# Slices of 1024 for the experts' weights, squares on ScalarE and another order of products in the first FFN chunk

## The chip, the core and the metric

The kernel runs on one core of one Trainium2 chip. The metric is the device time of one execution in microseconds. The kernel before takes 599.48 us, the median of 3 runs (598.98 to 600.8).

## The reference

Three stages follow each other: attention with four sink keys and a window of 128, a mixture of eight experts with one expert for each token, and an FFN with squared relu. In numpy, cut to what matters here:

```python
x = attention(q, k, v, n_sink, window)                   # (1536, 512)
expert_idx = np.argmax(x @ w_gate, axis=1)               # each token goes to one expert
h = np.maximum(np.einsum('ecd,edf->ecf', disp, w1), 0.0) # disp: the tokens of expert e; w1 (8, 512, 1024)
y = np.einsum('ecf,efd->ecd', h, w2)                     # w2 (8, 1024, 512)
out[i] = gate_w[i] * y[expert_idx[i], pos[i]]
r = np.maximum(out @ w_in, 0.0)                          # w_in (512, 2048), float64 in memory
return ((r * r) @ w_out).astype(np.float32)              # w_out (2048, 512), float64 in memory
```

## The kernel before

All products are done in pieces of float32 precision: every operand is kept as a high part (a cast to fp32r, made on ScalarE) and a low part (what the cast left, subtracted on VectorE), and three products are summed: high x high, high x low, low x high. So all weights have to be split before they are used, beside the products that run.

**Experts.** `body(e, b)` computes 128 tokens of expert e: `g1` (12 products for each half of the 1024 hidden columns), `relu` (L927), `tr` (four transposes, then hTh cast on ScalarE, L938, and hTl subtracted on VectorE, L939), `g2` (24 products into y), then ys = y x gate on VectorE (L981) and an indirect DMA on the POOL queue that scatters ys into yd (L982). Block 0 of each expert is a full body; `more` adds block 1 and 2 under a branch if the expert has more than 128 or 256 tokens. In the full body of expert e the weights of expert e + 1 are split: eight slices of 128x1024 (four of w1, four of w2), in 16 halves of 512. `split` casts a half on ScalarE (L144, into xh or yh; experts of even number are x, of odd number y) and subtracts on VectorE (L145, into xl or yl). The table HEAVY says how many halves stand at each of six places in the body; what is left comes last. `pre` transposes the tokens of the next blocks and splits them (xT0, xT1; L707, L708).

**Buffers.** Raw weights lie in six slots of 128x1024 float32 (tiles raw). A slot is free when the subtraction that reads it is done, and the SP queue then issues the next load in a fixed order: weights of experts, then the pieces of w_in and w_out.

**FFN.** w_in and w_out come as float64 words. A piece (128 rows x 1024 values, two slots, 1 MB) is converted in four steps (`piece_stage`): 0, ScalarE scales the high words (L180) and VectorE shifts the low words (L181); 1, two bit operations on VectorE (L183, L184); 2, ScalarE casts the high part (L186: xh for w_in, yh for w_out); 3, VectorE subtracts the low part (L188: xl, yl). One `tick` does 2 and 3 of the older piece and 0 and 1 of the newer, in the order 2, 0, 3, 1. The first three ticks lie in the last expert, the others one in each step of the first chunk of the FFN. The pieces come in the order i0, i1, o0, i2, o1, i3, ... o6, o7 (i: w_in, o: w_out).

The FFN takes 512 tokens at a time (three chunks). A step is one block of 128 hidden units: `stage_a` (12 products into a), relu on ScalarE (L1139), the square on VectorE (L1140), then `stage_g`: gh (or xT0h) cast on ScalarE (L1155), gl (or xT0l) subtracted on VectorE (L1157); then a tick if pieces are left, in some steps a transposed block of the next chunk (L1040, L1045, L1046), and `stage_b` of the step before: for each of four token tiles the products gh x yh, gh x yl, gl x yh (L1196), each tile in a PSUM bank of its own. A step's stage_b needs the piece of w_out whose steps 2 and 3 were done one step earlier or before.

All queues work in the order in which the code issues. On SP stand, at the head of the FFN, 12 writes of zeros into the output (L1116), then three loads of yd (L1034), between the loads of pieces.

Of the kernel before, what the change touches and what calls it, by code (L numbers as in the profile page):

```python
# [8 lines left out]
F32 = mybir.dt.float32  # L9
# [3 lines left out]
AF = mybir.ActivationFunctionType  # L13
# [3 lines left out]
P = 128  # L17
# [1 line left out]
NOBODY = 8192  # L19
NWARM0 = 10  # L20

HEAVY = (3, 1, 2, 2, 0, 4)
LIGHT = (1, 1, 1, 1, 1, 1)
LAST = (0, 0, 1, 0, 1, 1)
NWARM = 2
PTACT = (0, 2)
SPOOL = ()
SDVE = ()
FILL = {0: 4, 1: 4, 2: 2, 3: 2}


# [1 line left out]
def kernel(  # L33
# [15 lines left out]
    nc = tc.nc  # L49
# [8 lines left out]
    NFF = FF // P  # L58
# [56 lines left out]
    def freed(n=1):  # L115
        nonlocal held
        held -= n
        if eager:
            pull(NRAW)

    class Weights:
# [19 lines left out]
        def split(self, n, eng=None, hi=None):  # L141
            i, sl = n // 2, slice(n % 2 * 512, n % 2 * 512 + 512)
            t = self.raw[i]
            (hi or nc.scalar.copy)(self.h[i][:, sl], t[:, sl])  # L144
            (eng or nc.vector).tensor_sub(self.l[i][:, sl], t[:, sl], self.h[i].bitcast(F32)[:, sl])  # L145
            if n % 2:
                freed()

# [754 lines left out]
    def body(e, b, splits, plan, also):  # L905
        xh, xl = xT[e, b]
        wts = W[e]
        splits = list(splits)

        def sp(n):  # L910
            for _ in range(n):
                if splits:
                    splits.pop(0)()

        hs = mp.tile([P, F], F32, tag="hs", name="hs", bufs=1)
        hp = [None, None]

        def g1(half, ks):
            if ks[0] == 0:
                hp[half] = ps("s" if half or b else "iv", "h")  # L920
            for kk in ks:
                r = slice(half * 512, half * 512 + 512)
                for m, (a, bb) in enumerate(((xh, wts.h), (xh, wts.l), (xl, wts.h))):
                    nc.tensor.matmul(hp[half], a[:, kk, :], bb[kk][:, r], start=(kk == 0 and m == 0), stop=(kk == KD - 1 and m == 2))

        def relu(half):
            nc.scalar.activation(hs[:, half * 512 : half * 512 + 512], hp[half], AF.Relu)  # L927

        hT = [None, None]

        def tr(half):
            p_ = ps("pt", "hT")
            for c in range(4):
                o0 = half * 512 + c * P
                nc.tensor.transpose(p_[:, c * P : (c + 1) * P], hs[:, o0 : o0 + P], ident)
            h_ = mp.tile([P, 512], F32R, tag="hTh", name="hTh", bufs=2)
            l_ = mp.tile([P, 512], F32R, tag="hTl", name="hTl", bufs=2)
            nc.scalar.copy(h_, p_)  # L938
            nc.vector.tensor_sub(l_, p_, h_.bitcast(F32))  # L939
            hT[half] = (h_, l_)  # L940

        y = ps("ot", "y")

        def g2(fs):
            for f in fs:
                h_, l_ = (x[:, (f % 4) * P : (f % 4 + 1) * P] for x in hT[f // 4])
                wh, wl = wts.h[KD + f // 2], wts.l[KD + f // 2]
                r = slice((f % 2) * 512, (f % 2) * 512 + 512)
                for m, (a, bb) in enumerate(((h_, wh), (h_, wl), (l_, wh))):
                    nc.tensor.matmul(y, a, bb[:, r], start=(f == 0 and m == 0), stop=(f == NF - 1 and m == 2))  # L950

        def point(i):
            for f in also.get(i, ()):
                f()

        plan = iter(plan)
        g1(0, [0, 1, 2, 3])
        sp(next(plan))
        relu(0)
        g1(1, [0, 1])  # L960
        sp(next(plan))
        tr(0)
        g1(1, [2, 3])
        sp(next(plan))
        relu(1)
        point(0)
        g2([0, 1])
        sp(next(plan))
        tr(1)
        point(1)  # L970
        g2([2, 3])
        point(2)
        sp(next(plan))
        g2([4, 5])
        point(3)
        g2([6, 7])
        point(4)
        sp(next(plan))
        y_ = mp.tile([P, DM + 1], F32, tag="ys", name="ys", bufs=2)
        nc.gpsimd.tensor_copy(y_.bitcast(I32)[:, DM:], src[:, b, e : e + 1])  # L980
        nc.vector.tensor_scalar(y_[:, :DM], y, gate_at(e, b), None, op0=ALU.mult)  # L981
        nc.gpsimd.indirect_dma_start(  # L982
            out=yd[:, :], out_offset=bass.IndirectOffsetOnAxis(ap=dst[:, b, e : e + 1], axis=0), in_=y_, in_offset=None,
            bounds_check=NTOK - 1, oob_is_err=False,
        )
        sp(len(splits))
# [25 lines left out]
    stream += [(2, lambda p_=p_: piece_load(p_)) for p_ in order]  # L1012
    eager = True
    pull(NRAW)

    def split_at(g, i):
        W[g].split(i, nc.gpsimd if i in SPOOL else None, nc.vector.tensor_copy if i in SDVE else None)


    CH = 512  # L1020
# [54 lines left out]
    for e in range(E):  # L1075
        g = e + 1
        if e > 0:
            W[g].alloc()
        for b in range(1, XB):
            load_x(e + 1, b)  # L1080
        if g < E:
            splits = [(lambda i=i, g=g: split_at(g, i)) for i in range(16)]
        else:
            splits = [ticks.tick] * (NPRE + 1)
            its = load_y(0, ("bg", "bg"))
        if nblk:
            also = {2: [lambda: pre(e, 1), lambda: pre(e + 1, 0), lambda: load_x(e + 2, 0)]}
            also[4] = its[:-1]
            body(e, 0, splits, HEAVY if g < E else LAST, also)
            if nblk > 1:  # L1090
                vals[e] = nc.values_load(cnt[0:1, e : e + 1], min_val=0, max_val=cap)
            more(e, 1, its[-1:])
        else:
            for f in splits + its:
                f()
# [25 lines left out]
    def stage_a(c, f):  # L1121
        nonlocal its
        if f == 0:
            its = load_y(c + 1, ("pt", "ot")) if c + 1 < NCH else []
        a_ = ps("bg", "a")
        xh, xl = x2T[c]
        w = width[c]
        prods = []
        for kk in range(KD):
            r = slice(f % 2 * 512 + kk * P, f % 2 * 512 + kk * P + P)  # L1130
            wh, wl = WI.h[f // 2][:, r], WI.l[f // 2][:, r]
            prods += [(wh, xh[:, kk, :w]), (wl, xh[:, kk, :w]), (wh, xl[:, kk, :w])]
        if (c, f) == (0, 0):

            prods = [x for i, x in enumerate(prods) if i % 3 < 2] + prods[2::3]
        for i, (a, bb) in enumerate(prods):
            nc.tensor.matmul(a_[:, :w], a, bb, start=i == 0, stop=i == len(prods) - 1)  # L1137
        r_ = xring[f % 2, last][:, :w]
        nc.scalar.activation(r_, a_[:, :w], AF.Relu)  # L1139
        nc.vector.tensor_mul(r_, r_, r_)  # L1140
        gT[c, f] = r_


# [33 lines left out]
    def stage_b(c, f, only=None):  # L1177
# [4 lines left out]
            outp[c] = [ps("s" if t < 3 else "iv", "out") for t in range(nt)]  # L1182
        wh, wl = WO.h[f // 2], WO.l[f // 2]
        r = slice((f % 2) * 512, (f % 2) * 512 + 512)
        for t in blocks(c) if only is None else [only]:
            cs = slice(t * P, min(w, (t + 1) * P))
            rows = cs.stop - cs.start
            o = outp[c][t]
# [109 lines left out]
```

## Time and profile before

| | |
|---|---|
| median of 3 runs | 599.48 us |
| the profiled execution's own time | 599.34 us |
| its span, first to last instruction | 597.6 us |
| TensorE (PE) busy | 571.6 us, 96% |
| VectorE (DVE) busy | 354.2 us, 59% |
| ScalarE (ACT) busy | 296.7 us, 50% |
| GpSimd (POOL) busy | 138.8 us, 23% |
| granted TensorE clock, mean | 0.998 |

The span is some 1.7 us shorter than the execution's own time. Attention fills the first 131 us, the experts run to 322 us, the first chunk of the FFN to about 418 us, the other two to the end. Busy shares are averages over these parts. A row of a timeline gives the start, the duration, the engine, the line and operation with its tiles, and in brackets how long the engine was idle before it and what ended that.

### The profile page before, as it was taken

The page shows a single profiled execution, that of the slowest core. Times are in us where ns is not written, and L with a number is a line of the kernel's source. Part 1 is how long each engine was busy: PE and PEld are TensorE (multiplying, and loading weights), DVE is VectorE, ACT ScalarE, POOL GpSimd, SP SyncE. Part 2 cuts the span into 40 slices and gives each one's busy share as a digit, 9 for nine tenths or more (in the row PEclk, how much of TensorE's full clock was granted, in tenths as well). Part 3 has the DMA queues.
Part 4 walks back from the last instruction along what each step waited for, and adds up shares of the span by engine and source line. Part 5 has one row for each costly group of instructions (what it writes and reads, how often), then busy time and mean ns, then how long its engine had stood idle before and what let it go on. Part 6 is the DMA issues. An engine that isn't in the chain of part 4 may idle for free. (4 is left out here: it accounts for less than half of the span.)

```text
span 597.6 us, 9362 instructions
## 1 busy us (share of the span) xinstructions
PE 571.6 (96%) x3245; PEld 456.2 (76%) x3247; DVE 354.2 (59%) x838; ACT 296.7 (50%) x649; POOL 138.8 (23%) x235
## 2 busy tenths in 40 slices
PE   8999999989999999999899999999999999999994
PEld 4777777777887787777687677777888888888893
DVE  3788888758258857957853889886222232322222
ACT  4888888747247757737533455463222122222221
POOL 8544454244134413422111100000200000200002
PEclk9999999999999999999999999999999999999999
DMA  9688997457338975957731964521100000100001
GB/s 184 172 216 157 223 193 170 111 156 246 125 95 285 325 253 166 310 164 243 231 109 53 366 216 149 206 87 53 71 0 19 0 1 1 74 1 2 0 1 61
DMA packets 74625, 82.09 MB, mean 137 GB/s; under 512 B 42200, under 2 KB 53464, under 8 KB 74560
## 3 DMA queue, kind: packets, MB, share of 16 engines
q1 hardware_dynamic: 70608, 72.45, 41.8%
q0 software_dynamic: 3952, 8.82, 4.2%
q8 instruction: 35, 0.57, 0.4%
q14 instruction: 30, 0.25, 0.1%
HBM read 69.29 MB, written 16.08 MB: 143 GB/s over the span
## 5 line engine op out<-in xcount | busy, mean ns | idle before, releaser
L1140 DVE TENSOR_TENSOR xb<-xb 128x512 f32<-128x512 f32 (+1 forms) x48 | 31.6, 659 | 103.2 <-ACT xb L1139 103.2
L1139 ACT ACTIVATE xb<-a 128x512 f32<-128x512 f32 (+1 forms) x48 | 27.5, 573 | 111.8 <-PE a L1137 111.7
L454 ACT ACTIVATE p<-p,nm 128x260 f32<-128x260 f32 (+2 forms) x96 | 46.8, 489 | 17.3 <-DVE nm L442 16.0
L982 POOL DMA_INDIRECT yd<-ys,dst x14 | 26.3, 1881 | 114.3 <-DVE xl L145 32.5
L1163 POOL DMA_INDIRECT out_dram<-raw,tok x12 | 11.8, 986 | 168.8 <-issue 69.1
L1137 PE MATMUL a<-x2Ah,xh 128*128 128x512 f32 (+1 forms) x128 | 47.9, 374 | 0.3 <-PEq L1100 0.3
L1137 PE MATMUL a<-x2Ah,xl 128*128 128x512 f32 (+1 forms) x128 | 47.8, 374 | 0.0
L1137 PE MATMUL a<-x2Al,xh 128*128 128x512 f32 (+1 forms) x128 | 47.4, 374 | 0.0
L1196 PE MATMUL out<-yl,xT0h 128*128 128x512 f32 (+1 forms) x96 | 38.6, 402 | 4.9 <-DVE yl L188 4.9
L145 DVE TENSOR_TENSOR yl<-raw,yh 128x512 fp32r<-128x512 f32 x64 | 40.2, 686 | 4.6 <-ACT yh L144 4.1
L1196 PE MATMUL out<-yh,xT0h 128*128 128x512 f32 (+1 forms) x96 | 38.8, 405 | 0.4 <-ACT yh L186 0.4
L144 ACT CAST yh<-raw 128x512 fp32r<-128x512 f32 x64 | 35.3, 622 | 3.7 <-DVE off L1063 1.8
L1196 PE MATMUL out<-yh,gh 128*128 128x512 f32 (+1 forms) x92 | 36.4, 395 | 0.0
L1196 PE MATMUL out<-yl,gh 128*128 128x512 f32 (+1 forms) x92 | 36.3, 395 | 0.0
L144 ACT CAST xh<-raw 128x512 fp32r<-128x512 f32 x64 | 36.1, 619 | 0.3 <-ACTq L994 0.3
L939 DVE TENSOR_TENSOR hTl<-hT,hTh 128x512 fp32r<-128x512 f32 x28 | 19.3, 690 | 27.7 <-ACT hTh L938 27.7
L1196 PE MATMUL out<-yh,xT0l 128*128 128x512 f32 x88 | 34.8, 396 | 0.0
L1196 PE MATMUL out<-yh,gl 128*128 128x512 f32 x85 | 33.7, 396 | 0.0
L145 DVE TENSOR_TENSOR xl<-raw,xh 128x512 fp32r<-128x512 f32 x48 | 30.1, 686 | 1.9 <-ACT xh L144 1.8
L529 PE MATMUL ot<-pts,v 128*64 128x128 f32 x352 | 30.1, 286 | 0.5 <-ACT pts L496 0.5
L1155 ACT CAST xT0h<-xb 128x512 fp32r<-128x512 f32 (+1 forms) x24 | 14.3, 596 | 30.7 <-DVE xb L1140 30.7
L1155 ACT CAST gh<-xb 128x512 fp32r<-128x512 f32 (+1 forms) x23 | 13.7, 596 | 31.9 <-DVE xb L1140 31.9
(235 smaller groups left out, 1537.4 us busy)
## 6 DMA issues: line engine op xcount, KB each, us to landing
raw<-in_moe_w_dram SPq DMA_DIRECT2D x64, 512.0 KB, 5.7
raw<-in_moe_w_in_dram SPq DMA_DIRECT2D x16, 512.0 KB, 4.9
raw<-in_moe_w_out_dram SPq DMA_DIRECT2D x8, 1024.0 KB
yd<-zero SPq DMA_DIRECT2D x12, 256.5 KB, 5.4
xd<-x SPq DMA_DIRECT2D x12, 256.5 KB, 5.5
xb<-yd SPq DMA_DIRECT2D x12, 256.5 KB
kr<-in_k_dram SPq DMA_DIRECT2D x12, 256.0 KB, 4.7
qr<-in_q_dram SPq DMA_DIRECT2D x12, 256.0 KB, 7.3
```

The lines of the kernel that those rows point to most:

```text
L144: (hi or nc.scalar.copy)(self.h[i][:, sl], t[:, sl])
L145: (eng or nc.vector).tensor_sub(self.l[i][:, sl], t[:, sl], self.h[i].bitcast(F32)[:, sl])
L454: nc.scalar.activation(d["p"][:, h, :width], d["p"][:, h, :width], AF.Exp, bias=d["nm"][:, h : h + 1], scale=-1.0, accum_out=d["sm"][:, h ...
L529: nc.tensor.matmul(d["o"][i * D : (i + 1) * D, c * P : (c + 1) * P], vt[b, kb][:, h, :], t_, start=i not in d["started"], stop=False, skip ...
L939: nc.vector.tensor_sub(l_, p_, h_.bitcast(F32))
L982: nc.gpsimd.indirect_dma_start(out=yd[:, :], out_offset=bass.IndirectOffsetOnAxis(ap=dst[:, b, e : e + 1], axis=0), in_=y_, in_offset=None ...
L1137: nc.tensor.matmul(a_[:, :w], a, bb, start=i == 0, stop=i == len(prods) - 1)
L1139: nc.scalar.activation(r_, a_[:, :w], AF.Relu)
L1140: nc.vector.tensor_mul(r_, r_, r_)
L1155: nc.scalar.copy(gh[:, :w], r_)
L1163: i = nc.gpsimd.indirect_dma_start(out=out, out_offset=bass.IndirectOffsetOnAxis(ap=tok[:rows, n : n + 1], axis=0), in_=o_[:rows, :], in_o ...
L1196: nc.tensor.matmul(o, a, bb[:, r], start=(f == 0 and m == 0), stop=(f == NFF - 1 and m == len(prods) - 1))
```

## The change

The eight slices of an expert's weights are split whole (128x1024) instead of in halves, at seven places of the body, one of them new (behind `tr(1)`). While pieces are left to convert, the square is done on ScalarE. In the first chunk, while pieces are left, stage_b does all four tiles' gh x yh first, then all gl x yh, then all gh x yl.

```diff
-HEAVY = (3, 1, 2, 2, 0, 4)
-LIGHT = (1, 1, 1, 1, 1, 1)
-LAST = (0, 0, 1, 0, 1, 1)
+HEAVY = (2, 0, 1, 1, 1, 1, 2)
+LIGHT = (0, 0, 0, 0, 0, 0, 0)
+LAST = (0, 0, 1, 0, 0, 1, 1)
 NWARM = 2
 PTACT = (0, 2)
-SPOOL = ()
-SDVE = ()
...
+        def split_slice(self, i):
+            nc.scalar.copy(self.h[i], self.raw[i])
+            nc.vector.tensor_sub(self.l[i], self.raw[i], self.h[i].bitcast(F32))
+            freed()
...
         g2([0, 1])
         sp(next(plan))
         tr(1)
+        sp(next(plan))
         point(1)
...
-            splits = [(lambda i=i, g=g: split_at(g, i)) for i in range(16)]
+            splits = [(lambda i=i, g=g: W[g].split_slice(i)) for i in range(8)]
...
         nc.scalar.activation(r_, a_[:, :w], AF.Relu)
-        nc.vector.tensor_mul(r_, r_, r_)
+
+        if ticks.done():
+            nc.vector.tensor_mul(r_, r_, r_)
+        else:
+            nc.scalar.activation(r_, r_, AF.Square)
         gT[c, f] = r_
...
-        for t in blocks(c) if only is None else [only]:
+        ts = blocks(c) if only is None else [only]
+        if not ticks.done() and c == 0 and f < NFF - 1:
+
+            for a, bb in ((gh, wh), (gl, wh), (gh, wl)):
+                for t in ts:
+                    nc.tensor.matmul(
+                        outp[c][t], a[:, t * P : (t + 1) * P], bb[:, r], start=(f == 0 and a is gh and bb is wh), stop=False
+                    )
+            return
+        for t in ts:
```

The order of VectorE's instructions in a full body, here that of expert 0, from the second hTl on (yl and yh are the next weights' low and high parts; the numbers are buffers). Before:

```order
L939 TENSOR_TENSOR hTl<-hT,hTh 128x512
L708 TENSOR_TENSOR xT1l<-xT,xT1h 128x512
L712 TENSOR_SCALAR gate_202<-xb_207 128x1
L713 RECIPROCAL gate_202<-gate_202 128x1
L708 TENSOR_TENSOR xT0l<-xT,xT0h 128x512
L712 TENSOR_SCALAR gate_200<-xb_205 128x1
L713 RECIPROCAL gate_200<-gate_200 128x1
L145 TENSOR_TENSOR yl_3210<-raw_76,yh_3209 128x512 x2
L145 TENSOR_TENSOR yl_3212<-raw_76,yh_3211 128x512 x2
L981 TENSOR_SCALAR ys<-y,gate_199 128x512
L145 TENSOR_TENSOR yl_3214<-raw_74,yh_3213 128x512 x2
L145 TENSOR_TENSOR yl_3216<-raw_74,yh_3215 128x512 x2
```

and with the change:

```order
L942 TENSOR_TENSOR hTl<-hT,hTh 128x512
L149 TENSOR_TENSOR yl_3178<-raw_76,yh_3177 128x1024
L711 TENSOR_TENSOR xT1l<-xT,xT1h 128x512
L715 TENSOR_SCALAR gate_202<-xb_207 128x1
L716 RECIPROCAL gate_202<-gate_202 128x1
L711 TENSOR_TENSOR xT0l<-xT,xT0h 128x512
L715 TENSOR_SCALAR gate_200<-xb_205 128x1
L716 RECIPROCAL gate_200<-gate_200 128x1
L149 TENSOR_TENSOR yl_3180<-raw_76,yh_3179 128x1024
L149 TENSOR_TENSOR yl_3182<-raw_74,yh_3181 128x1024
L149 TENSOR_TENSOR yl_3184<-raw_74,yh_3183 128x1024
L985 TENSOR_SCALAR ys<-y,gate_199 128x512
```

One slice has moved ahead of xT1l, and ys now stands behind all slices, where two of them stood behind it. ScalarE's casts moved in the same way.

ScalarE in one step of the first chunk and the relu of the next (xb is the step's tile of relu and square, raw the pieces). Before:

```order
L1139 ACTIVATE xb_205<-a 128x512
L1155 CAST xT0h<-xb_205 128x512
L186 CAST yh_5325<-raw_74 128x1024
L180 ACTIVATE raw_75<-raw_75 128x1024
L1139 ACTIVATE xb_209<-a 128x512
```

and with the change:

```order
L1140 ACTIVATE xb_205<-a 128x512
L1145 ACTIVATE xb_205<-xb_205 128x512
L1160 CAST xT0h<-xb_205 128x512
L189 CAST yh_5213<-raw_74 128x1024
L183 ACTIVATE raw_75<-raw_75 128x1024
L1140 ACTIVATE xb_209<-a 128x512
```

The square has come in between relu and cast; on VectorE its row is gone.

TensorE in stage_b, behind the last product of a stage_a. Before (first tile, and the first product of the second):

```order
L1137 MATMUL a<-x2Al,xh_4909 128x512
L1196 MATMUL out<-yh_5323,gh_5343 128x512
L1196 MATMUL out<-yl_5324,gh_5343 128x512
L1196 MATMUL out<-yh_5323,gl_5344 128x512
L1196 MATMUL out<-yh_5323,gh_5343 128x512
```

and with the change (all four tiles, and the next stage_a):

```order
L1195 MATMUL out<-yh_5215,xT0h 128x512 x4
L1195 MATMUL out<-yh_5215,xT0l 128x512 x4
L1195 MATMUL out<-yl_5216,xT0h 128x512 x4
L1138 MATMUL a<-x2Ah,xh_4801 128x512
L1138 MATMUL a<-x2Ah,xl_4802 128x512
```

The products with yl, which were each tile's second, are now the last four; behind them the next stage_a begins.

## Rows read from the trace of the kernel before

**Rows 1.** Timeline of TensorE, first chunk; start us, duration us, engine, line, operation [idle before]

```profile
322.20 0.47 PE L1137 MATMUL a<-x2Ah,xh 128*128 128x512 f32 x1 [0.30 <-PEq L1100]
...
341.10 0.50 PE L1196 MATMUL out<-yl,xT0h 128*128 128x512 f32 x1 [0.93 <-DVE yl L188]
...
404.34 0.50 PE L1196 MATMUL out<-yl,xT0h 128*128 128x512 f32 x1 [0.92 <-DVE yl L188]
```

**Rows 2.** Timeline of ScalarE, the relus of two steps behind the last piece

```profile
415.67 0.60 ACT L1139 ACTIVATE xb<-a 128x512 f32<-128x512 f32 x1 [3.59 <-PE a L1137]
...
421.27 0.60 ACT L1139 ACTIVATE xb<-a 128x512 f32<-128x512 f32 x1 [3.62 <-PE a L1137]
```

**Rows 3.** Timeline of VectorE, one step of the first chunk

```profile
355.90 0.68 DVE L1140 TENSOR_TENSOR xb<-xb 128x512 f32<-128x512 f32 x1
357.27 0.69 DVE L1157 TENSOR_TENSOR gl<-xb,gh 128x512 fp32r<-128x512 f32 x1 [0.69 <-ACT gh L1155]
357.88 0.69 DVE L181 TENSOR_SCALAR raw<-raw 128x1024 int32<-128x1024 int32 x1
358.48 1.22 DVE L188 TENSOR_TENSOR xl<-raw,xh 128x1024 fp32r<-128x1024 f32 x1
359.62 1.22 DVE L183 SCALAR_TENSOR_TENSOR raw<-raw 128x1024 int32<-128x1024 int32 x1
360.87 1.23 DVE L184 SCALAR_TENSOR_TENSOR raw<-raw 128x1024 int32<-128x1024 int32 x1
362.02 0.68 DVE L1140 TENSOR_TENSOR xb<-xb 128x512 f32<-128x512 f32 x1
```

**Rows 4.** Timeline of ScalarE, the same step

```profile
356.62 0.62 ACT L1155 CAST gh<-xb 128x512 fp32r<-128x512 f32 x1 [2.91 <-DVE xb L1140]
357.14 1.13 ACT L186 CAST xh<-raw 128x1024 fp32r<-128x1024 f32 x1
358.18 1.18 ACT L180 ACTIVATE raw<-raw 128x1024 f32<-128x1024 f32 x1
```

**Rows 5.** Timeline of TensorE, first products of three full bodies and one wait

```profile
169.45 0.39 PE L924 MATMUL h<-yh,xT0h 128*128 128x512 f32 x1
...
182.68 0.47 PE L924 MATMUL h<-xh,xT0h 128*128 128x512 f32 x1
...
187.44 0.63 PE L935 MATMUL hT<-ident,hs 128*128 128x128 f32 x4 [0.33 <-ACT yh L144]
...
197.44 0.47 PE L924 MATMUL h<-yh,xT0h 128*128 128x512 f32 x1
```

**Rows 6.** Waits from 170 to 285 us: for whom; us in total, times, longest

```profile
PE y L950 <- DVE hTl L939: 2.0, 3, 0.7
```

**Rows 7.** Timeline of VectorE, full bodies that begin at 169.45 and 182.68

```profile
179.96 0.69 DVE L708 TENSOR_TENSOR xT1l<-xT,xT1h 128x512 fp32r<-128x512 f32 x1 [1.09 <-ACT xT1h L707]
...
187.45 2.50 DVE L145 TENSOR_TENSOR yl<-raw,yh 128x512 fp32r<-128x512 f32 x4 [0.21 <-ACT yh L144]
189.87 0.68 DVE L939 TENSOR_TENSOR hTl<-hT,hTh 128x512 fp32r<-128x512 f32 x1
```

**Rows 8.** Timeline of ScalarE, the cast that this hTl needs

```profile
188.11 0.59 ACT L938 CAST hTh<-hT 128x512 fp32r<-128x512 f32 x1 [0.70 <-PE hT L935]
```

**Rows 9.** Busy time by stretch: us, PE, PEld, DVE, ACT, POOL, PEclk, DMA share, GB/s

```profile
322.00:412.00 90.00, 84.42 (x362) 66.36 (x363) 76.73 (x87) 46.30 (x60) 5.42 (x5) 1.00 0.55 187
328.00:346.00 18.00, 16.64 (x71) 12.86 (x70) 15.46 (x18) 9.12 (x13) 2.55 (x3) 1.00 1.06 367
```

**Rows 10.** Timeline of VectorE, a wait for a piece of w_out

```profile
345.65 0.70 DVE L181 TENSOR_SCALAR raw<-raw 128x1024 int32<-128x1024 int32 x1 [0.22 <-DMA raw<-in_moe_w_out_dram]
```

**Rows 11.** Timeline of TensorE, first transposes of blocks read from yd, last expert

```profile
294.08 0.66 PE L1040 MATMUL x2T<-ident,xb 128*128 128x128 f32 x4 [1.61 <-DMA xb<-yd]
```

**Rows 12.** Timeline of POOL, two scatters

```profile
159.24 1.00 POOL L982 DMA_INDIRECT yd<-ys,dst  x1 [8.33 <-DVE ys L981]
...
282.15 2.54 POOL L982 DMA_INDIRECT yd<-ys,dst  x1 [10.21 <-issue]
```

More of the change, by code (lines that the diff above doesn't have):

```diff
@@ L1014 @@
     pull(NRAW)
-    def split_at(g, i):
-        W[g].split(i, nc.gpsimd if i in SPOOL else None, nc.vector.tensor_copy if i in SDVE else None)
     CH = 512
```

## The prediction

> **What bounds the kernel now.** I read the page first: TensorE is busy for 96% of the span, so a gain can only come from the places where it waits. Next I looked for idle marks in TensorE's own timeline. Behind the attention part they stand in three places: in the first chunk of the FFN, in expert bodies that follow another full body at once, and at the end of the last expert's first body.
>
> *FFN, first chunk.* Six times TensorE waits for the low half of a piece of w_out, first and last in [rows 1]. What it should take is read where nothing is converted any more: one step (stage_a and stage_b, 24 products) is 5.60 us from relu to relu [rows 2], so each half is 2.80 and a product 0.233. From the start at 322.20 [rows 1] to the relu at 421.27 [rows 2] stand 17 stage_a, 15 stage_b and four groups of transposes of about 0.36: 32 x 2.80 + 1.4 = 91.0, to 413.2. The chunk loses 8.0 us. The cause is VectorE [rows 3]: from one squaring to the next 6.12 us pass with one gap only, 0.69, in which it waits for ScalarE's cast of the square. It is slower than TensorE's 5.60, and 6.7 in steps with transposes. ScalarE has room [rows 4].
>
> *Experts.* The body that begins at 169.45 takes 13.23 us to the next; the one that follows it 14.76 (182.68 to 197.44) [rows 5]. In it TensorE waits for the first hT transposes (0.33) and for hTl, with the refill behind each wait some 1.4 in all. Three bodies show the wait for hTl, 2.0 us together, 0.7 at most [rows 6]: 3 x 1.4 = 4.2 us. [rows 7, 8] show why: hTh is cast by 188.70, but VectorE is in four halves of the next weights and begins hTl at 189.87, 1.17 late.
>
> **The change, part by part.** Durations are of the profiled execution, 599.34 us; the median of the three runs is 599.48, 0.14 more.
>
> *Squares to ScalarE.* VectorE loses the 1.37 us from squaring to gl [rows 3] in 14 steps: 6.12 - 1.37 = 4.75, and 5.35 with the low half of a transposed block. ScalarE gains a square of 128x512. No row shows it; the bounds are 0.52 (the cast's spacing, 356.62 to 357.14) and 0.69 (VectorE's own). I take 0.60, a relu's duration. ScalarE's step becomes relu 0.60, square 0.60, cast 0.52, weights' cast 1.04, scaling 1.18: 3.9 [rows 4], with the transposed block's cast 4.5. Both stay below 5.60, so TensorE sets the pace: price nothing, covered by 0.85 of slack on VectorE; if that cover goes, a step again takes VectorE's time.
>
> *Low halves' products last.* In a step, counted from the end of stage_a: relu to 0.60, square 1.20, gh 1.8, gl 2.5, shift 3.1, low half of the piece 4.3. stage_b that reads it starts at 5.6. So the new order is not needed in the usual step; it gives the low half another 7 x 0.233 = 1.63 us. It changes the accumulating bank at each product instead of at each third, at the same number of products: nothing.
>
> *What is late next.* From 328 to 346 the DMA engines are full (share 1.06, 367 GB/s) [rows 9]: the writes of zeros, three pieces, and blocks of yd. VectorE waits there for a piece of w_out that lands at 345.65 [rows 10]. Its load sits in SP's queue behind the zeros and is not moved by the change, but the work that needs it is: in step 3 stage_a ends near 339.2, so VectorE would now reach the shift at 341.7 and ScalarE the scaling at 342.1, and both queues stand still until 345.65. Behind the scaling is the relu of step 4, due at 344.8 and now done from 346.8. Then VectorE: shift 0.60, subtraction 1.13, two bit operations 1.25 and 1.23, to 349.9; ScalarE's cast of the piece to 351.0. stage_b of step 4 could begin at 322.2 + 10 x 2.80 = 350.2: TensorE waits 0.8. The low half is there at 352.3; in the old order its first product would come at 351.2, a further 1.1 of waiting, in the new one at 351.0 + 8 x 0.233 = 352.9. Here, and only here, the order pays. Sum for the FFN: 8.0 - 0.8 = 7.2, rounded down to 7.0 for refills; if the piece lands with the next one (1.1 later) 5.9; if nothing stalls 8.0.
>
> *Slices of 1024.* A subtraction of 1024 takes a spacing of 1.14 (358.48 to 359.62) [rows 3] against two halves at 0.61 (four run from 187.45 to 189.87) [rows 7], ScalarE 1.04 against about 1.07 for two. So between xT1l and the next hTl, 12 halves (7.3 us) become five slices (5.7), and a sixth moves ahead of xT1l, where VectorE sat idle for 1.09 [rows 7] and overruns by 0.45: 7.3 - 5.7 - 0.45 = 1.15 gained against 1.17 late. The wait for hTl goes. On ScalarE the relu stands behind two slices instead of three halves, but one slice has gone ahead of the xT casts, so it starts some 0.5 earlier; and nothing stands between it and the transposes now, where TensorE was released only by the end of the half cast behind it [rows 5]. The wait of 0.33 goes. Together 4.2; a slice in front of a small operation can hold it 1.14 instead of 0.61, so I take 3.6, with bounds 1.8 (half) and 4.2. The first bodies of a chain have slack: nothing.
>
> *The block's result waits for two slices more.* ys now stands behind all eight slices: 2 x 1.14 later, less some 0.8 gained ahead of it, 1.5 us. Queued behind it are POOL's scatter of the block and the later reads of xb there. Their readers come a body later, but in the last expert the reads of yd wait for expert 6's scatter: TensorE waits 1.61 us for them and goes on at 294.08 [rows 11]. POOL's scatter takes 2.54 there, beside VectorE's subtractions, and 1.00 at 159.24, where VectorE is idle [rows 12]; with ys last VectorE is idle behind it. So it starts 1.5 later and takes 1.5 less: I take 0, with -1.5 (no shorter) and +1.2 (the scatter comes ahead of the piece's traffic) as bounds. The Trainium skill, GPSIMD Engine Reference, section Specifications, says that GpSimd's SBUF interfaces are shared with VectorE, with contention from instructions of two SBUF inputs; the 2.54 and 1.00 agree, and by that rule the sum would have 0 here, without it -1.5.
>
> The last expert's own stall (0.3 at its first transposes) is swallowed by the wait at 294.08: nothing. SP's order of loads is unchanged.
>
> **Sum.** 7.0 + 3.6 + 0 = 10.6: 599.34 - 10.6 = 588.7, on the median's footing 588.9, said as **589.0**.
>
> **Rivals.** *A, half of it.* The piece lands later (5.9), the expert chains keep half their waits (1.8), the scatter costs 1.5: 6.2, **593.3**. For it speak DMA engines that are full exactly there; against it VectorE's slack in all later steps. *B, all of it.* 8.0 + 4.2 + 1.2 = 13.4: **586.1**. *C, the loads decide.* The chunk's steps stay bound by the pieces: only the experts gain, and the scatter costs 1.5 and more, 2 left: **597.5 to 599**. Against it: outside 328 to 346 a piece of 1 MB at 367 GB/s needs 2.9 of 5.60 us. *D, slower: long slices in front of short operations.* In all seven full bodies hTh, hTl and the relu come a half slice (0.53) later with no slack: 3 x 0.53 x 7 = 11.1, plus the scatter's 1.5 and no gain in the chains: -12.6 + 7.0 = 5.6 slower, **605**. It decides if over half of these delays reach TensorE; against it, bodies outside a chain show no such wait: of eight, three have it [rows 6]. *E, slower: the clock.* If changing banks at each product let TensorE fall from 2.4 to 1.2 GHz in the 12 reordered stage_b, 144 products at another 0.233 cost 33.6: **623**. The granted clock is 1.00 in that stretch [rows 9], with a change of bank at each third product. The Trainium skill, TensorE: Matmul & The Clock Gate, section A second HAM failure mode: psum-queue depth-cycling, tells of a kernel that cycled through banks and lost its clock; the trace here speaks against it. That the change doesn't do what it says is not open: the order of instructions shows each part.
>
> **How the numbers follow.** The forecast, 586.5 to 591.0, gets 0.62; A (to 595.5) 0.24; B 0.06; C 0.03; D 0.04; E 0.01. A measurement of this kernel tells some 0.3%, 1.8 us, from no change. Faster is forecast, A and B: 0.92; C 0.03 the same; D and E 0.05 slower. The range leaves out C, D, E and the ends of A and B: 586.0 to 594.0.
>
> **What would show it.** In the changed profile: relus of the first chunk 5.6 apart but for one pause near 346; VectorE with gaps in each of its steps; no wait for yl at the products; one wait of some 0.8 for the cast of a piece; bodies of 13.3 us in chains; scatters of about 1 us behind ys. It is wrong if VectorE still fills its steps, if waits for hTh or hTl appear in bodies that had none, or if the reads of yd come later than now.

## The result, and the profile after

The changed kernel takes 589.95 us, the median of 4 runs (589.29 to 591.8); the kernel before took 600.14 us in the same job (4 runs, 598.98 to 600.82). The ratio is 0.9831, with a 95% interval of 0.9806 to 0.9856, about 10 us. The forecast was 589.0. The profiled execution takes 589.9 us, its span is 588.2 us, 9.4 less than before.

Page, busy time and share of each engine:

```profile
PE 569.4 (97%) x3247; PEld 456.5 (78%) x3247; DVE 342.1 (58%) x768; ACT 302.2 (51%) x607; POOL 128.9 (22%) x235
```

Timeline of TensorE, first products of bodies and of the first chunk, and its only wait in the chunk:

```profile
182.81 0.47 PE L927 MATMUL h<-xh,xT0h 128*128 128x512 f32 x1
...
187.08 0.60 PE L938 MATMUL hT<-ident,hs 128*128 128x128 f32 x4
...
196.36 0.48 PE L927 MATMUL h<-yh,xT0h 128*128 128x512 f32 x1
...
275.62 0.47 PE L927 MATMUL h<-yh,xT0h 128*128 128x512 f32 x1
...
289.47 0.66 PE L1041 MATMUL x2T<-ident,xb 128*128 128x128 f32 x4 [0.86 <-DMA xb<-yd]
290.60 0.63 PE L1041 MATMUL x2T<-ident,xb 128*128 128x128 f32 x4 [0.47 <-DMA xb<-yd]
292.22 0.66 PE L1041 MATMUL x2T<-ident,xb 128*128 128x128 f32 x4 [0.99 <-DVE x2Al L1047]
...
318.29 0.47 PE L1138 MATMUL a<-x2Ah,xh 128*128 128x512 f32 x1 [0.30 <-PEq L1101]
...
347.72 0.50 PE L1195 MATMUL out<-yh,xT0h 128*128 128x512 f32 x1 [1.19 <-ACT yh L189]
```

The body that follows a full body takes 13.55 us (182.81 to 196.36) where it took 14.76 [rows 5]; its transposes at 187.08 carry no wait, and none of the waits for hTl is left that [rows 6] counted. The chunk starts 3.91 earlier than in [rows 1]. The six waits for yl are gone; one for the cast yh has come.

VectorE, one step and the wait behind it (answers to [rows 3] and [rows 10]):

```profile
331.96 0.69 DVE L1162 TENSOR_TENSOR xT0l<-xb,xT0h 128x512 fp32r<-128x512 f32 x1
332.57 0.69 DVE L184 TENSOR_SCALAR raw<-raw 128x1024 int32<-128x1024 int32 x1
333.26 1.23 DVE L191 TENSOR_TENSOR yl<-raw,yh 128x1024 fp32r<-128x1024 f32 x1
334.41 1.22 DVE L186 SCALAR_TENSOR_TENSOR raw<-raw 128x1024 int32<-128x1024 int32 x1
335.66 1.23 DVE L187 SCALAR_TENSOR_TENSOR raw<-raw 128x1024 int32<-128x1024 int32 x1
337.31 0.69 DVE L1162 TENSOR_TENSOR gl<-xb,gh 128x512 fp32r<-128x512 f32 x1 [0.43 <-ACT gh L1160]
342.26 0.70 DVE L184 TENSOR_SCALAR raw<-raw 128x1024 int32<-128x1024 int32 x1 [4.25 <-DMA raw<-in_moe_w_out_dram]
```

ScalarE, the same stretch (answers to [rows 2] and [rows 4]):

```profile
335.36 0.60 ACT L1140 ACTIVATE xb<-a 128x512 f32<-128x512 f32 x1 [1.08 <-PE a L1138]
335.99 0.64 ACT L1145 ACTIVATE xb<-xb 128x512 f32<-128x512 f32 x1
336.66 0.62 ACT L1160 CAST gh<-xb 128x512 fp32r<-128x512 f32 x1
337.19 1.13 ACT L189 CAST xh<-raw 128x1024 fp32r<-128x1024 f32 x1
342.26 1.19 ACT L183 ACTIVATE raw<-raw 128x1024 f32<-128x1024 f32 x1 [3.94 <-DMA raw<-in_moe_w_out_dram]
343.32 0.59 ACT L1140 ACTIVATE xb<-a 128x512 f32<-128x512 f32 x1
...
346.52 1.15 ACT L189 CAST yh<-raw 128x1024 fp32r<-128x1024 f32 x1 [1.28 <-DVE raw L187]
```

VectorE no longer has the square; it fills its steps while pieces have to be caught up, first near the chunk's start and again from 342 to 367, and has a gap of 0.6 to 0.8 in each step from there on. The square (L1145) takes 0.64 on ScalarE, and the relu at 335.36 waits for TensorE (1.08), as it should. Both engines then stand until 342.26, and the relu at 343.32 comes 7.96 behind the last.

Busy time by stretch, columns as in [rows 9], shifted by the 4 us by which the chunk starts earlier:

```profile
318.00:408.00 90.00, 88.53 (x387) 71.25 (x388) 69.99 (x76) 58.05 (x76) 1.88 (x5) 1.00 0.56 187
324.00:342.00 18.00, 18.00 (x79) 14.50 (x78) 13.35 (x15) 11.22 (x15) 0.55 (x3) 1.00 1.04 352
```

Though more of the work falls into the 90 us (387 matmul records, not 362), VectorE is busy for 6.7 us less in them, and ScalarE, which has the squares, for 11.8 more. The DMA engines are as full in the second stretch as before (1.04 against 1.06), and the granted clock is 1.00.

**Where the 9.4 us come from.** This is the difference of two profiles, one execution of each kernel. Three bodies in chains: 14.76 to 13.55, 14.43 to 13.18, 14.45 to 13.20, together 3.7. The last expert's first body: 17.44 to 17.13, 0.3. The first chunk, from its start to the relu of the next: 99.07 (322.20 to 421.27) to 93.08 (318.29 to 411.37), 6.0. Against that stand 0.1 ahead of 182.81 and 0.5 behind the chunk, of which 0.4 lies in two steps between 502.67 and 512.94 that the profiles of three variants below (e3, e7, e10) don't show.

### The profile page after: what moved, and what is told of

It reads as the page before. It is cut to its first block, busy times and chain, and to the rows that moved or that the text cites. A ratio compares the mean times of both kernels' runs of the same rounds, so it can differ in the third digit from the quotient of the medians.

```text
span 588.2 us, 9240 instructions
## 1 busy us (share of the span) xinstructions
PE 569.4 (97%) x3247; PEld 456.5 (78%) x3247; DVE 342.1 (58%) x768; ACT 302.2 (51%) x607; POOL 128.9 (22%) x235
## 5 line engine op out<-in xcount | busy, mean ns | idle before, releaser
L1168 POOL DMA_INDIRECT out_dram<-raw,tok x12 | 11.8, 984 | 168.3 <-issue 69.2
L149 DVE TENSOR_TENSOR yl<-raw,yh 128x1024 fp32r<-128x1024 f32 x32 | 38.1, 1223 | 3.0 <-ACT yh L148 2.6
L148 ACT CAST yh<-raw 128x1024 fp32r<-128x1024 f32 x32 | 32.4, 1051 | 4.0 <-DVE off L1064 1.8
L930 ACT ACTIVATE hs<-h 128x512 f32<-128x512 f32 x28 | 16.7, 597 | 29.6 <-PE h L927 29.5
L941 ACT CAST hTh<-hT 128x512 fp32r<-128x512 f32 x28 | 16.4, 587 | 28.0 <-PE hT L938 22.0
L149 DVE TENSOR_TENSOR xl<-raw,xh 128x1024 fp32r<-128x1024 f32 x24 | 28.6, 1222 | 1.9 <-ACT xh L148 1.3
L495 PE MATMUL pt<-ident,p 128*128 128x128 f32 x176 | 28.0, 278 | 0.8 <-ACT pts L499 0.3
L1210 PE MATMUL out<-yl,xT0h 128*128 128x512 f32 (+1 forms) x72 | 28.4, 395 | 0.0
L1138 PEld LDWEIGHTS a<-x2Ah,xh 128*128 128x128 f32 x128 | 24.0, 188 | 4.6 <-issue 1.0
L894 POOL DMA_INDIRECT xb<-xd,src x23 | 24.9, 1085 | 11.0 <-issue 4.6
L1138 PEld LDWEIGHTS a<-x2Ah,xl 128*128 128x128 f32 x128 | 24.0, 188 | 3.7
```

Of the source, the lines that this page charges most:

```text
L148: nc.scalar.copy(self.h[i], self.raw[i])
L149: nc.vector.tensor_sub(self.l[i], self.raw[i], self.h[i].bitcast(F32))
L495: nc.tensor.transpose(p_[:, x * P : (x + 1) * P], d["p"][:, h, c0 : c0 + P], ident)
L894: nc.gpsimd.indirect_dma_start(out=x_at(e, b), out_offset=None, in_=xd[:, :], in_offset=bass.IndirectOffsetOnAxis(ap=src[:, b, e : e + 1], ...
L1210: nc.tensor.matmul(o, a, bb[:, r], start=(f == 0 and m == 0), stop=(f == NFF - 1 and m == len(prods) - 1))
```

## The experiments

Theory: each part gives what its own term says, squares the FFN's gain, slices and places the experts'. Rivals: the order of products carries the FFN's gain, the size of a slice or its places alone the experts', and at the last expert the scatter, a load or something else decides. Ratios are to the kernel before in the same job.

### The FFN: the order of products, and the squares

Old order of products, squares still on ScalarE:

```diff
-        if not ticks.done() and c == 0 and f < NFF - 1:
+        if False and not ticks.done() and c == 0 and f < NFF - 1:
```

> The changed kernel, but stage_b keeps the old order of products (each tile: gh x yh, gh x yl, gl x yh). My theory (the square on ScalarE gives the chunk back to TensorE, the order pays at one place only): no wait for yl in any usual step; in the one stage_b after the late piece TensorE waits for yh as now (1.2) and then for yl about 1.1 more; the first chunk takes 91.1 us from the first relu to the next chunk's first relu instead of 90.0; total about 591. Rival (the order is what removed the six waits for yl): the waits come back in every second step, 0.3 to 0.9 each, the chunk takes 94 or more, total about 594.

Measured: 591.87 us, 0.9855 (0.9833 to 0.9878). Its chunk, from first relu to the next chunk's first, takes 90.84 where the change has 90.01. Timeline of TensorE in this kernel:

```profile
350.00 0.51 PE L1210 MATMUL out<-yh,xT0h 128*128 128x512 f32 x1 [0.99 <-ACT yh L189]
351.25 0.50 PE L1210 MATMUL out<-yl,xT0h 128*128 128x512 f32 x1 [0.76 <-DVE yl L191]
```

The wait for yl comes back at one place, behind the late piece, and nowhere else: the order is worth 0.8 there, and nothing in the usual step. In this execution the piece landed 23.76 us behind the chunk's start, 0.21 earlier than with the change; without that the difference would be 1.0 by estimate (0.83 + 0.21), near the 1.1 that was said. The profiled execution is 2.9 longer than that of the change: 0.8 is the chunk, 0.7 a wait for a relu in the body that begins at 196.06 (under the experts, below), and 2.0 the last expert's two bodies, where TensorE waits longer and the clock falls (last section), less 0.7 at other places.

Squares back on VectorE, new order kept:

```diff
-        if ticks.done():
+        if True or ticks.done():
             nc.vector.tensor_mul(r_, r_, r_)
```

> The changed kernel, but the square stays on VectorE; the new order of products is kept. My theory: VectorE is full again (6.1 us a step, 6.7 with a transposed block), so the chunk takes 95 to 96 us instead of 90.0 and TensorE waits for other things than yl (gl, or the cast yh); total about 595. Rival (the order does it): the chunk takes 91 to 92, total about 591.

Measured: 598.02 us, 0.9969 (0.9941 to 0.9997); chunk 96.42, against 96.00 before. Timeline of TensorE in this kernel:

```profile
350.46 1.20 PE L1195 MATMUL out<-yh,xT0h 128*128 128x512 f32 x4 [1.48 <-ACT yh L189]
...
375.52 1.20 PE L1195 MATMUL out<-yh,xT0h 128*128 128x512 f32 x4 [0.92 <-ACT yh L189]
```

With VectorE over its step, the wait only moves from yl to yh, whose cast needs VectorE's bit operations. The order alone gives none of the chunk's gain. The squares alone give 5.2 of it (96.00 to 90.84 in e1), and the order adds its 0.8 once VectorE is free. The total is 3.0 above what was expected; the chunk is 0.4 longer than said, and the profile shows 0.7 of the excess in a wait for a relu (body at 196.17) and 1.5 in the last expert's second body, behind a fall of the clock.

### The experts: size or place

Old experts with the new FFN (16 halves at the old places):

```diff
-HEAVY = (2, 0, 1, 1, 1, 1, 2)
+HEAVY = (3, 1, 2, 2, 0, 0, 4)
...
-            splits = [(lambda i=i, g=g: W[g].split_slice(i)) for i in range(8)]
+            splits = [(lambda i=i, g=g: W[g].split(i)) for i in range(16)]
```

> The changed kernel with the experts' splits as before (halves, old places): only the FFN part of the change. My theory (the two parts add): the experts' bodies show the old waits for hT and hTl and end 4.0 us later than in the changed kernel, the first chunk takes 90 us as there; total about 594. Rival (the experts' part only moves a wait, so that one part alone gives nearly all): 590 to 591, or 598.

Measured: 593.43 us, 0.9888 (0.9857 to 0.9919). The old waits for hT and hTl are back (0.33 and 0.66), the bodies take 14.76, 14.42 and 14.47, as before. So the FFN's part does nothing to the experts. The chunk takes 88.95 here, 1.06 less than with the change and than expected, because the piece of w_out lands 22.91 us behind the chunk's start (23.97 with the change) and TensorE does not wait for it. That the slower experts cause this is not shown: in e4, whose bodies are slow too, it lands 24.30 behind the start. No run has the experts' part alone.

Halves at the new places:

```diff
-HEAVY = (2, 0, 1, 1, 1, 1, 2)
+HEAVY = (4, 0, 2, 2, 2, 2, 4)
...
-            splits = [(lambda i=i, g=g: W[g].split_slice(i)) for i in range(8)]
+            splits = [(lambda i=i, g=g: W[g].split(i)) for i in range(16)]
```

> The changed kernel, but the experts' weights split in halves of 512, at the new places (4, 0, 2, 2, 2, 2, 4). My theory (place and size each give part): VectorE saves 0.08 a pair less, so between xT1l and the next hTl it is about 0.6 later than now; TensorE waits for hTl some 0.3 to 0.5 in each of the three bodies that follow a full body, 1 to 1.5 us in all; total about 591. Rival 1 (the size does it all): the old waits, +3.7, 593.6. Rival 2 (the places do it all): no wait, 590.

Slices of 1024 at the old places:

```diff
-HEAVY = (2, 0, 1, 1, 1, 1, 2)
+HEAVY = (2, 0, 1, 1, 0, 2, 0)
```

> The changed kernel, but the slices of 1024 at the old places: none ahead of the xT casts, ys between the sixth and the seventh slice. My theory: VectorE loses the 0.65 that the slice ahead of xT1l gave, and hTl is about 0.5 late in each of the three bodies, with the refill 0.6 each, 1.8 us; ys comes earlier, but POOL's scatter takes 2.5 again beside a subtraction; total about 592. Rival 1 (the places do it all): the old waits, 593.6. Rival 2 (the size does it all): 590.

Measured: halves at the new places 589.07 us, 0.9838 (0.9802 to 0.9874), bodies 13.59, 13.28 and 13.26; slices at the old places 594.18 us, 0.9898 (0.988 to 0.9916), bodies 14.37, 14.04 and 14.05. VectorE with halves at the new places:

```profile
186.44 2.50 DVE L143 TENSOR_TENSOR yl<-raw,yh 128x512 fp32r<-128x512 f32 x4 [0.21 <-DVEq L998]
188.86 0.68 DVE L942 TENSOR_TENSOR hTl<-hT,hTh 128x512 fp32r<-128x512 f32 x1
```

TensorE with slices at the old places, in the first body of the three:

```profile
190.18 0.50 PE L953 MATMUL y<-xh,hTl 128*128 128x512 f32 x1 [0.48 <-DVE hTl L942]
```

So my theory for the halves fell: they lose nothing, and the second rival held. The places alone give 1.2 for each chained body, the size alone 0.4, and both together at most 0.1 more than the places. Of the two places that moved, it is the slice ahead of xT1l that counts: e8 (below) has ys ahead of two slices again, and two of its three chained bodies take 13.56 and 13.21 without a wait. The total with slices at the old places is 2.2 above what was said: the three bodies lose 2.5, not 1.8, and the last expert's two bodies take 32.1 instead of 30.2, with a fall of the clock in the second.

A wait that the profile of the change does not have comes with the same expert code in others. In the body that begins near 196 the load of a slice is late, the cast of that slice stands ahead of the relu on ScalarE, and TensorE waits for the relu at the first transposes: 0.69 (e1), 0.67 (e2), 0.85 (e9), 1.01 (e10), 0.24 (e11), and 0.65 in e8; no wait shows in the change and in e7. ScalarE and TensorE in e10:

```profile
199.99 1.05 ACT L148 CAST xh<-raw 128x1024 fp32r<-128x1024 f32 x1 [1.55 <-DMA raw<-in_moe_w_dram]
...
201.59 0.66 PE L938 MATMUL hT<-ident,hs 128*128 128x128 f32 x4 [1.01 <-ACT hs L930]
```

Busy time in that stretch, columns as in [rows 9], before and with the change:

```profile
196.00:210.00 14.00, 12.88 (x62) 9.79 (x61) 12.66 (x23) 10.88 (x22) 6.28 (x5) 1.00 0.91 320
196.00:210.00 14.00, 13.85 (x67) 11.05 (x67) 13.36 (x18) 11.61 (x15) 5.06 (x5) 1.00 0.99 346
```

The DMA engines were at 0.91 there and are full with the change (0.99), and a load that comes late reaches TensorE: the 3.7 us of the chains are 2.6 in the profile of e10. With halves (e3, e12, e13) a cast waits up to 0.65 for a load there too, and TensorE does not wait; whether the size is the reason was not tested.

### The late piece

The zeros issued on SP ahead of the last expert's second body instead of at the head of the FFN:

```diff
             body(e, 0, splits, HEAVY if g < E else LAST, also)
+            if e == E - 1:
+                zf = zb.bitcast(F32)
+                zw = zf.shape[1]
+                for t in range(NQB):
+                    nc.sync.dma_start(
...
-    for t in range(NQB):
-        nc.sync.dma_start(
```

> The changed kernel with the 12 writes of zeros issued in the last expert, behind its first body, where the DMA engines are nearly idle, instead of at the head of the FFN. My theory (the last wait of the chunk is the piece of w_out that comes late because the zeros are ahead of it): the 4 us pauses of VectorE and ScalarE for that piece go, TensorE's wait for yh (1.2) goes, the chunk takes 88.2 to 88.6 us; total about 588.5. Rival (the piece is late for another reason, its own load or SP's order): the wait stays at 0.8 or more, the chunk takes 89.5 to 90.

Measured: 589.41 us, 0.983 (0.9798 to 0.9861). The chunk takes 88.55 with no wait for a piece: the zeros in SP's queue are what makes it late, and the late piece costs the change 1.46. The total shows little of it. The profile has a stretch at half the clock in the last expert, and the mean clock of the four runs is 0.990 to 0.994, against 0.994 to 0.997 for the change. Timeline of TensorE there:

```profile
292.10 0.66 PE L1041 MATMUL x2T<-ident,xb 128*128 128x128 f32 x4 [1.71 <-DVE x2Al L1047]
...
293.19 0.39 PE L927 MATMUL h<-yh,xT1l 128*128 128x512 f32 x1
293.43 0.50 PE L927 MATMUL h<-yh,xT1h 128*128 128x512 f32 x1
293.72 0.63 PE L927 MATMUL h<-yl,xT1h 128*128 128x512 f32 x1
294.15 0.63 PE L927 MATMUL h<-yh,xT1l 128*128 128x512 f32 x1
```

Busy time by stretch in the same kernel (the granted clock is the third number from the end):

```profile
293.00:297.00 4.00, 4.00 (x12) 3.12 (x11) 3.56 (x4) 2.51 (x3) 0.00 (x0) 0.57 0.45 121
```

From 293.6 to 297.0 products stand up to 0.43 apart, not 0.233: seven lose 0.195 each and two at the ends some 0.2 together, 1.5 us, and the body takes 14.55 instead of 13.02.

### The last expert

ys ahead of the last two slices, to see whether the scatter decides there:

```diff
-HEAVY = (2, 0, 1, 1, 1, 1, 2)
+HEAVY = (2, 0, 1, 1, 1, 1, 0)
```

> The change, but ys stands ahead of the last two slices of an expert's weights (before, two of four 512-halves stood behind it). Theory: what ys gains in place the scatter loses in length, because VectorE subtracts beside it: ys about 2.3 us earlier, scatter of expert 6 some 2.5 us instead of 1.04, so the reads of yd come at most 0.8 us earlier and the whole is the same within 0.8 us (589.2 to 590.7). Rival: the scatter takes 1.0 us there too; the reads come 2.3 us earlier, the waits for blocks of yd (0.86 and 0.47) go, and the whole takes 588.3 us or less.

Measured: 589.91 us, 0.9835 (0.9809 to 0.9861). Timeline of POOL, expert 6's scatter:

```profile
278.02 1.26 POOL L986 DMA_INDIRECT yd<-ys,dst  x1 [9.42 <-DVE ys L985]
```

VectorE beside that scatter, and later, in the last expert's first body:

```profile
277.16 2.35 DVE L149 TENSOR_TENSOR yl<-raw,yh 128x1024 fp32r<-128x1024 f32 x2
...
288.13 1.23 DVE L191 TENSOR_TENSOR xl<-raw,xh 128x1024 fp32r<-128x1024 f32 x1
289.28 1.21 DVE L186 SCALAR_TENSOR_TENSOR raw<-raw 128x1024 int32<-128x1024 int32 x1
290.52 1.23 DVE L187 SCALAR_TENSOR_TENSOR raw<-raw 128x1024 int32<-128x1024 int32 x1
291.67 1.28 DVE L1047 TENSOR_TENSOR x2Al<-x2T,x2Ah 128x512 fp32r<-128x512 f32 x2
```

TensorE, its one wait for these blocks:

```profile
292.41 0.66 PE L1041 MATMUL x2T<-ident,xb 128*128 128x128 f32 x4 [2.73 <-DVE x2Al L1047]
```

The scatter takes 1.26 with VectorE subtracting beside it, not 2.5, and the blocks of yd land 12.0 us behind the body's start (288.10, POOL's read of the first) instead of 13.9. ys comes 2.3 us earlier, as said, but the rest of my theory's reason is wrong, the scatter's length and the time of the reads, and yet the total is the same: the waits for the DMA become one of 2.73 for VectorE. The blocks' low halves (x2Al) stand in its queue behind the second tick's conversions, which end some 15.7 us into the body in both kernels (e8 at 291.67, 276.06 + 15.6; the change at 291.48, 275.62 + 15.9), whatever the reads do.

So I moved the blocks: the first three into the second body (e9), and that with the zeros earlier (e10):

```diff
-            also[4] = its[:-1]
...
-            more(e, 1, its[-1:])
+            more(e, 1, its[:-1], its[-1:])
```

> The changed kernel with the first three transposed blocks of yd moved from the end of the last expert's first body into its second, and the fourth into its third. My theory (TensorE's 2.9 us there are only the way from the scatter of expert 6 to the loads of yd): the waits for xb and x2Al go, the first body of the last expert takes 13.1 instead of 17.1 and the second 14.1 instead of 13.0; total about 587. Rival (the conversions of pieces on VectorE are what is late, and follow): a wait of 1 us or more for x2Al or xb stays in the second body; total 589 to 590.

> The changed kernel with both: the zeros issued behind the last expert's first body, the blocks of yd transposed in its second and third. Expected, if the two are independent: 1.5 + 2.9 less than the changed kernel, about 585.5. Rival: the fourth block's load stands behind the zeros in SP's queue, and TensorE waits for it in the third body, some 3 us; total 588 to 589.

Measured: 592.21 us, 0.9865 (0.9835 to 0.9895), and 588.68 us, 0.9806 (0.9787 to 0.9826). In e9 the first body falls to 12.56 and the second rises to 16.83; the rival held there, with waits of 1.52 for the relu and 1.08 for x2Al in the second body. The total is above its 589 to 590, because the piece comes later still (a wait of 1.99) and the clock falls behind that wait (chunk 92.33). In e10 the chunk is 88.56, but the bodies take 13.26 and 16.82, 30.08 together against 30.15: the stall has moved. Its rival gave the right total by a wait that doesn't come; TensorE waits for nothing in the third body. ScalarE in e10:

```profile
292.90 1.14 ACT L189 CAST xh<-raw 128x1024 fp32r<-128x1024 f32 x1 [3.06 <-DVE raw L187]
293.93 1.16 ACT L183 ACTIVATE raw<-raw 128x1024 f32<-128x1024 f32 x1
294.97 0.59 ACT L930 ACTIVATE hs<-h 128x512 f32<-128x512 f32 x1
```

The second body's relu stands behind a tick's cast that waits for VectorE's bit operations. Then the third tick was moved behind the second body (e11), the same with halves (e12), and behind the branch that follows (e13):

```diff
-            splits = [ticks.tick] * (NPRE + 1)
+            splits = [ticks.tick] * NPRE
...
             more(e, 1, its[:-1], its[-1:])
+            if e == E - 1:
+                ticks.tick()
```

> As e10_both, and the third tick of the float64 weights (high and low part of i1, first steps of o0) is issued behind the last expert's second body instead of at the end of its first. Theory: the loss at the last expert comes from a relu that queues on ScalarE behind that tick's casts (in e10_both the second body took 16.82 us, with 3.06 us of waiting on ScalarE for the conversion); without it the second body takes some 13.5 us, so the first chunk starts about 3 us earlier and the whole takes 585.7 us. Rival 1: the pieces are then late instead, TensorE waits in the first two steps of the chunk for what the tick makes or for the next piece (its slots come free 3 us later), the body gets shorter but the chunk longer by as much: 588.7 us. Rival 2: the blocks of yd, not the conversions, hold the second body: it stays at 16 to 17 us, 588.7 us.

> As e11_third_tick_later, and the experts' weights split in halves of 512 at the new places (as in e3_halves_new_places). Theory: the size of a slice doesn't matter once the places are right, so the same as e11_third_tick_later within 0.6 us. Rival: slices of 1024 spare VectorE 0.08 us a pair and ScalarE the end of a half in front of the relu, so halves are 1 to 2 us slower.

> As e12_tick_later_halves, and the third tick stands behind the branch that reads blocks of yd again when few tokens lie ahead of the last expert (L1109 there), no longer in front of it. Theory: in e11 and e12 TensorE waited 3.07 and 2.69 us in step 0 because VectorE's queue reaches that branch only after the tick's four conversions, and the wait brought a stretch at half the granted clock; with the branch ahead of the tick both go, the chunk starts about 40.9 us behind the last expert's first body and step 0 takes 2.8 us: 587.2 us. Rival: what the tick makes, or the blocks' gh and gl, is needed as soon, and VectorE, which comes free from ys only at about 317, makes TensorE wait as long at the first products with a piece of w_out: 590 to 591 us.

Measured: e11 591.85 us, 0.9862 (0.9841 to 0.9883); e12 590.91 us, 0.9859 (0.9837 to 0.988); e13 590.43 us, 0.9838 (0.982 to 0.9856). e12 is 0.9 below e11, where at most 0.6 was said; the runs of the two overlap (590.61 to 592.21, 590.88 to 592.26). In e11 the two bodies take 27.91, 2.2 less than with the change, and the chunk starts at 316.50 instead of 318.29. Then TensorE stands, in e11 in step 0, in e13 a little later, at the first stage_b, so the first rival of e11 held: the bodies are shorter and the chunk longer. Timeline of TensorE in e11, where VectorE's queue reaches the branch (L1109) only behind the tick:

```profile
321.69 2.08 PE L1140 MATMUL a<-x2Al,xh 128*128 128x512 f32 x4 [3.07 <-DVEq L1109]
```

TensorE in e13, at the first products with a piece of w_out:

```profile
325.06 2.08 PE L1196 MATMUL out<-yh,xT0h 128*128 128x512 f32 x4 [2.47 <-ACT xT0h L1161]
```

ScalarE in e13, the two instructions ahead of that xT0h's square:

```profile
322.09 1.11 ACT L189 CAST yh<-raw 128x1024 fp32r<-128x1024 f32 x1 [6.52 <-DVE raw L187]
323.10 0.59 ACT L1141 ACTIVATE xb<-a 128x512 f32<-128x512 f32 x1
```

In e13 the relu again, due when TensorE ends stage_a near 319.6, stands behind a cast that waits for VectorE's conversions; the rival of e13 held. Each of the three also has the clock at half behind that wait (0.66 or 0.83 on average from 320 to 330). Three ticks have to be fitted around two bodies, and at each place that was tried the conversions of one stand ahead of something TensorE needs. A tick in the middle of the second body, ahead of its relu's turn but behind its cast, was not tried. No variant is shown to beat the change: the interval of e10, the lowest, overlaps that of the change, though its four runs (588.18 to 589.28) lie below all four of the change, in another job.

## Why the prediction was right, and where it was not

**FFN, said 7.0, came 6.0.** The mechanism held: squares off VectorE, relus 5.60 apart (6.03 in steps with transposes), one wait. VectorE has a gap in each step only behind 367, not in all of them, as was said. Two sizes were off. *What it should take* was counted as 91.0 us; with no wait at all it is 91.6 (e7: 319.70 to 411.31), mostly since each of the four groups of transposes costs 0.42, not 0.36, and the first relu comes 3.06 behind the start, not 2.80. And the *late piece*, said 0.8, cost 1.46: it landed 24.0 us behind the chunk's start (342.26 - 318.29), not 23.45, so the wait was 1.19, and the steps around it took the rest. This size is one execution's: the wait is 0.55, 0.99, 1.01, 1.19 and 1.53 where the piece lands 23.30, 23.76, 23.78, 23.97 and 24.30 behind the start (e3, e1, e8, the change, e4), and none where it lands at 22.91 (e5). 8.0 - 0.6 - 1.46 gives the 6.0 within 0.1. That it would be this piece, that the wait would be for the cast, and that the order pays there alone, held; e2 shows that the new order is nothing by itself.

**Experts, said 3.6, came 3.7, by another reason.** The step that failed is "7.3 - 5.7 - 0.45 = 1.15 gained against 1.17 late", which credited the size of a slice. e3 has halves and no wait. What the step overlooked stands in the waits: only 0.66 of the 1.17 us reached TensorE, as the first products behind the transposes need hTh alone; 1.17 - 0.66 = 0.51 of lateness is free. In e3 hTl begins 0.51 behind the end of hTh (188.86, against 187.76 + 0.59 on ScalarE), and TensorE does not wait. Two halves fewer behind xT1l are enough for that, and the new places leave nothing between relu and transposes. That 3.6 fits is luck in part: the waits with their refills were worth 1.24 each, not 1.4, so 3.7 is all of them, while 3.6 had been a deduction from 4.2 for long slices ahead of short operations. The change's profile has no such loss; in others the late load costs up to 1.0.

**The last expert, said 0 between -1.5 and +1.2, came +0.3.** Right in size by luck, wrong in its steps. The scatter of expert 6 did take 1.04 (from 279.85, VectorE idle) where it took 2.54 [rows 12], but an idle VectorE gives only 0.2 of that: e8 has 1.26 beside subtractions. What goes with the 2.54 is halves instead of slices right behind ys: at the old places the seven scatters beside them take 2.51 to 2.54 in e5 (halves) and 1.24 to 1.26 in e4 (slices). The Trainium skill, GPSIMD Engine Reference, section Specifications, says that GpSimd and VectorE share their SBUF interfaces, with contention from VectorE's instructions of two SBUF inputs. Subtractions are such instructions, but the rule alone doesn't give these sizes; e3 has 1.03 beside four halves, and the reason stays open. And the chain from scatter to read was not what bound. "TensorE waits 1.61 us for them" named the first of three waits; the last, in the kernel before, ends 2.06 behind it and is for VectorE:

```profile
296.14 0.66 PE L1040 MATMUL x2T<-ident,xb 128*128 128x128 f32 x4 [0.53 <-DVE x2Al L1046]
```

Behind the reads stood VectorE's second tick.

**Rivals.** A had the piece 1.1 later, and the late piece cost 0.7 more than said; its other two terms did not come. No run shows B's full 1.2 at the last expert without a tick less there. C did not come as it was put, the steps of the chunk are not bound by the pieces, but a little of it did in the experts, where the DMA engines are full from 196 to 210 and a late load costs TensorE up to 1.0 in other profiles. D did not come in the profile of the change: no body there shows a longer wait in front of hTh or a relu. E did not come: the clock in the reordered stretch is 1.00. There the Trainium skill's warning about cycling banks (TensorE: Matmul & The Clock Gate, section A second HAM failure mode: psum-queue depth-cycling) has no case in this trace: a new bank at each product cost nothing.

## What to carry to other kernels

When an edit changes both the size and the place of side work, try the place alone: which small operation on the path stands behind it mattered more here than its own length (1.2 us a body against 0.4). When a wait on a load is named, look at what stands behind that load in the other engines' queues before pricing its removal; here the next limit was 2 us behind the first. And a conversion that lags on one engine holds everything queued behind its partner on the other, so moving it moves the stall.

## What the runs showed of the hardware

The granted clock falls to half (1.2 GHz) behind the stall of the last expert, for 3.4 us, in the profiles of e1, e2, e4 and e7, and not in those of before, the change, e3, e5, e8, e9 and e10. It costs some 1.5 us (e7). TensorE's waits at that place don't tell them apart: e4 and e8 both wait 2.73 us once; e2 with the fall and the change without it have the same code there and wait 2.3 in three pieces each. The same 3.4 us follow the wait of 1.99 for the late piece in e9, while waits of 1.48 (e2) and 1.53 (e4) at that place are followed by none. So a wait that costs 2 us by its row may cost 3.5, in some executions only. This is worth as much as a term of the sum, and the runs of the change themselves go from 589.29 at a mean clock of 0.997 to 591.8 at 0.994.

POOL's scatter of 128 rows took 2.53 or 2.54 us at six places of the kernel before. With the change none takes over 1.73; beside subtractions that run all along it takes 1.03 (e3), 1.26 (e8) or 1.73, and with VectorE idle 0.98 to 1.04. VectorE's work beside it explains a part only.
